# Constant products in TensorE's early gaps, a third head pair turned in float32, and a new order

## The chip, the cores and the metric

One core of one Trainium2 chip. The metric is the device time of one execution in microseconds (us). A kernel's runs are compared by their median. PE stands for TensorE's matmuls, PEld for its weight loads, DVE for VectorE, ACT for ScalarE, POOL for GpSimd, SP for the queue that issues the DMAs.

## The reference, cut to what matters

```python
# q, k, v: (4, 8, 768, 64) float32; proj: (64, 6); w_in: (512, 2048); w_out: (2048, 512)
q_bucket = sum((q @ proj > 0) * 2**arange(6)); k_bucket = the same of k
scores = where(q_bucket == k_bucket, q @ k.T / 8, -1e9)
attn = softmax(scores)              # per batch and head, 768 x 768
x = (attn @ v) as (3072, 512)       # heads side by side
h = x @ w_in
out = (0.5 * h * (1 + erf(h / sqrt(2)))) @ w_out
```

## The kernel before, in words

The work is a list of steps, each with an engine (or several that it may run on), a cost, a sort key out of the table `PAR`, and the steps that it needs. `Plan.order()` walks through them event by event and fixes the order in which every engine's instructions are written; the loop at the end of `tile_bucket_attention_moe` then emits them. On the chip each engine works through its own list in that order and waits on semaphores. So numbers in `PAR` and `HOPX` alone can move any step to another place or engine.

Attention is done in 192 **units**: one head, 128 rows of queries. A unit is: scores on TensorE (`scores`, L764, four matmuls, written to one of two PSUM buffers, s_62 or s_63, of two banks each); the row maximum on VectorE (L767); a guard (L771); the exponential with its row sum on ScalarE (L777); a reciprocal (L786). The weights must then be transposed for the product with the values, in one of two ways:

- *In halves:* VectorE or another engine writes a float16 high part (L396 or L399), VectorE the low part (L792), and the DMA queue transposes both (`turn`). The product with the values (L889) then has three float16 terms: 36 matmuls for two heads and 256 rows. The values too are split into halves (L631 is their low part).
- *Whole* (`whole_turn`): TensorE multiplies the float32 weights by a diagonal matrix of the reciprocals (L832, six matmuls for each unit), and ScalarE or VectorE copies the two halves of the result out of PSUM (`pt<-hp`, L396 or L399). The product with the values (L880) is in float32, 12 matmuls for two heads and 256 rows; the trace shows each float32 matmul as two records.

There are five passes over the units: pass one (rows 0 to 255 of batch 0, units 1 to 16), pass two (the other 512 rows of batch 0, units 17 to 48, the heads in reverse order), and one pass for each of the batches 1 to 3 (units 49 to 192). `WHOLE` says how many of the four head pairs of each pass go the whole way: four in pass one, two in pass two.

Before scores can be made, each head is hashed (`head`: copies, low parts, L719 to L724 on TensorE, signs on ScalarE). Beside the attention of batch 0 the two weight matrices are decoded out of float64 bits on VectorE (L488, L493, L498), their column sums come from TensorE (L510), and they are scaled and split (L558). The feed-forward part is written in groups: L1091 (into the hidden layer), GELU and split, L1158 (out of it). Its matmuls are the only large work that has no successor waiting; TensorE takes them wherever the plan puts them, and about a quarter of the span is left for them at the end, when no attention is left.

The planner keeps a model of TensorE's clock: time is counted in windows, and a step costs double while the window before was not busy enough (`warm`, `window`, `busy`).

Of the kernel before, what the change touches and what calls it, by code (L numbers as in the profile page):

```python
# [24 lines left out]
NEARLY = 2  # L25
RAWE = 1
KEEP = 3
WHOLE = (4, 2, 0, 0, 0)
TABLE = 1.3
WORDER = (("in", 0), ("in", 1), ("out", 0), ("out", 1), ("in", 2), ("in", 3), ("out", 2), ("out", 3))  # L30
GROW = ("p", "hl", "hl", "hl")

PAR = dict(DR_ACT=-376.07, DR_DVE=289.34, SI0=-278.25, SI1=416.6, SI2=306.7, SI_ACT=509.76, SI_DVE=47.66, SI_Pool=-124.88, Z=203.87, VS0=-105.38, H0=492.56, HL=-258.56, VS=-598.47, G2=553.48, HQ=415.51, VQ=-319.5, in0=576.69, out0=43.64, in1=45.59, out1=-9.06, in2=355.85, out2=56.84, in3=-68.45, out3=9.31, H1=322.83, H2=284.27, H3=-599.77, H4=-314.36, H5=134.87, H6=-600, H7=-32.98, MEV=599.38, MGE=18.26, MSP=118.02, V0=600, QK0=-74.85, QK1=593.04, QK2=76.57, MX0=-331.22, MX1=-185.25, MX2=-453.28, EX0=-301.14, EX1=-117.73, EX2=94.64, NR0=-107.13, NR1=-107.34, NR2=-398.77, HI0=584.08, HI1=-88.77, HI2=215.64, LO0=-593.61, LO1=-36.26, LO2=394.43, PV0=336.47, PV1=233.76, PV2=-154.35, TR0=-587.53, TR1=-414.23, TR2=158.02, V1=-484.38, V2=-573.42, Sin0=304.53, Sin1=397.8, Sin2=24.49, Sin3=-283.57, Sout0=471.96, Sout1=295.43, Sout2=26.22, Sout3=336.14, Lin=-221.37, Pin=-423.65, Qin=587.63, Cin=107.98, Min=438.2, Lout=-519.34, Pout=-600, Qout=-600, Cout=-600, Mout=578.13, G0=109.59, G1=-596.66, G3=-600, G4=-600, G5=-286.31, G6=-363.67, G7=-231.43, DUP0=-165.96, DUP1=326.7, DUP2=-339.67, LOW0=420.82, LOW1=-261.59, LOW2=-577.83, PRJ0=282.56, PRJ1=-69.75, PRJ2=-89.26, MSK0=456.41, MSK1=238.81, MSK2=501.82, DI_ACT=-410.83, DI_DVE=252.78, DI_Pool=-258.86, WS_ACT=-29.21, WS_DVE=-440.66, WS_Pool=490.46, WH_ACT=181.51, WH_DVE=-447.36, WH_Pool=-599.06, WL_ACT=70.41, WL_DVE=214, WL_Pool=283.28, VH_ACT=203.1, VH_DVE=477.67, VH_Pool=-442.09, MV_SP=97.35, MV_ACT=338.88, MV_DVE=-2.69, MV_Pool=-599.57, LO_ACT=301.58, LO_DVE=265.1, LO_Pool=-475.84, RND_ACT=-398.89, RND_DVE=200.27, RND_Pool=-52.67, MSK_ACT=48.02, MSK_DVE=-6.3, MSK_Pool=587.68, HI_ACT=-301.94, HI_DVE=128.62, HI_Pool=-390.82, DG_ACT=-447.94, DG_DVE=-318.17, DG_Pool=490.83, EV_ACT=140.3, EV_DVE=-346.2, EV_Pool=-344.6, GH_ACT=361.7, GH_DVE=587.31, GH_Pool=-257.89)
HOPX = {"PE": 0.0, "DVE": -0.1, "ACT": 0.14, "Pool": 0.1, "SP": 0.93}
BIG = 2.0**34
TINY = 2.0**-120

# [16 lines left out]
class Plan:  # L54
# [39 lines left out]
    def order(self):  # L94
# [26 lines left out]
        free_at.update(self.START)  # L121
        dma_at, table = 0.0, "exp"
        port_at, port_of = 0.0, None
        warm, window, busy = False, 0, {}
        mode = 0
        for t in set(free_at.values()):
            heapq.heappush(events, (t, -1, None))
# [1 line left out]
        while events:  # L129
            now, _, ended = heapq.heappop(events)  # L130
            batch = [ended]
            while events and events[0][0] <= now:
                batch.append(heapq.heappop(events)[2])
            for e in batch:
                if e is None:
                    continue
                for hold in e.frees:
                    hold["left"] -= 1
                    if not hold["left"]:
                        at_ = now + self.HOP[e.engine]  # L140
                        self.rings[hold["holder"].takes].append((hold["holder"].slot, at_))
                        heapq.heappush(events, (at_, -1, None))
                for u in users.get(e, ()):
                    left[u] -= 1
                    for w in u.ways:
                        hop = self.SAME.get(w, 0.05) if w == e.engine else self.HOP[e.engine] + HOPX.get(e.engine, 0.0) + 0.12 * (w == "Pool")
                        at[u, w] = max(at.get((u, w), 0.0), now + hop)
                        heapq.heappush(events, (at[u, w], -1, None))
                    if not left[u]:
                        enlist(u)  # L150
            for engine, pool in ready.items():
                if free_at[engine] > now or not pool:
                    continue
                best = None
                for s in pool:
                    if at.get((s, engine), 0.0) > now:
                        continue
                    if s.takes and not (self.rings[s.takes] and self.rings[s.takes][0][1] <= now):
                        continue
                    if engine == "SP" and len(s.ways) > 1 and dma_at > now + self.QUEUE:  # L160
                        continue
                    held = engine == "Pool" or (engine == "DVE" and s.port)
                    if held and port_of != engine and port_at > now:
                        continue
                    rank = (s.key + s.ways[engine][1], s.seq)
                    if best is None or rank < best_rank:
                        best, best_rank = s, rank
                if best is None:
                    continue
                s = best  # L170
                for e in s.ways:
                    ready[e].remove(s)
                s.engine, s.cost = engine, s.ways[engine][0]
                if s.takes:
                    s.slot = self.rings[s.takes].pop(0)[0]
                    head[s.takes] += 1
                    if head[s.takes] < len(queues[s.takes]):
                        after = queues[s.takes][head[s.takes]]
                        if after in waiting:
                            waiting.remove(after)  # L180
                            enlist(after)
                s.start = now
                cost = s.cost
                if s.table and s.table != table:
                    cost += TABLE
                    table = s.table
                if engine == "PE":
                    cost += self.SWITCH[mode][s.mode]
                    mode = s.mode
                    while window < int(now / self.WINDOW):  # L190
                        share = busy.get(window, 0.0) / self.WINDOW
                        warm = share > (0.35 if warm else 0.8)
                        window += 1
                    cost *= 1 if warm else 2
                    a, z = now, now + cost
                    while a < z:
                        w = int(a / self.WINDOW + 1e-9)
                        b = min(z, (w + 1) * self.WINDOW)
                        busy[w] = busy.get(w, 0.0) + b - a
                        a = b  # L200
                if engine == "SP":
                    free_at[engine] = now + s.issue
                    dma_at = max(dma_at, now + 1.0) + cost
                    if dma_at > now + self.QUEUE:
                        heapq.heappush(events, (dma_at - self.QUEUE, -1, None))
                    s.end = dma_at + 0.75
                else:
                    free_at[engine] = s.end = now + cost
                    if engine == "Pool" or (engine == "DVE" and s.port):
                        port_at, port_of = s.end - self.PORT, engine  # L210
                        heapq.heappush(events, (port_at, -1, None))
                count += 1
                heapq.heappush(events, (free_at[engine], -1, None))
                heapq.heappush(events, (s.end, s.seq, s))
# [8 lines left out]
def tile_bucket_attention_moe(  # L223
# [10 lines left out]
    nc = tc.nc  # L234
# [102 lines left out]
    ident = const.tile([P, P], BF16, tag="ident", name="ident")  # L337
    make_identity(nc, ident)
    ones = const.tile([P, P], BF16, tag="ones", name="ones")
    nc.gpsimd.memset(ones, 1.0)  # L340
    warm = const.tile([P, 1], F32, tag="warm", name="warm")
    nc.scalar.activation(out=warm, in_=ones[:, :1], func=AF.Exp)
    limit = const.tile([P, 2], F32, tag="limit", name="limit")
    nc.gpsimd.memset(limit, BIG / 2)
    SPARE = 1000
    for t in bufs["s"]:
        nc.vector.memset(t[:, SPARE : SPARE + 1], 1.0)

# [13 lines left out]
    for n, rr in enumerate((slice(0, D), slice(D, P))):  # L362
        nc.vector.tensor_tensor(
            out=hash_lo[rr, n * KR : n * KR + 2 * NBIT], in0=praw[rr],
            in1=hash_hi[rr, KR : KR + 2 * NBIT].bitcast(F32), op=ALU.subtract,
        )

    plan = Plan(rings)
# [594 lines left out]
    for n_pass, (b, chunks) in enumerate(passes):  # L963
# [9 lines left out]
        for pos, h in enumerate(heads):  # L973
# [14 lines left out]
            _, _, base, made = owner[i]  # L988
# [255 lines left out]
```

## Time and profile before

| | |
|---|---|
| median of 3 runs | 907.84 us (907.3 to 909.52) |
| the profiled execution | 907.79 us, of which 906.0 us are the span from the first instruction to the last |
| PE busy | 865.1 us, 95% |
| DVE busy | 693.8 us, 77% |
| ACT busy | 618.9 us, 68% |
| POOL busy | 275.4 us, 30% |
| mean granted TensorE clock | 0.987 |

The busy shares are means over two very different stretches: up to about 680 us attention runs, with the feed-forward part between its steps; after it only the feed-forward part is left, and the page's row of tenths shows VectorE at one or two tenths there.

### The profile page before, as it was taken

What the parts mean: (1) busy time and instruction counts of PE and PEld (TensorE: products, weight loads), DVE (VectorE), ACT (ScalarE), POOL (GpSimd) and SP (SyncE); (2) the same over time, 40 slices, a digit from 0 to 9 for tenths busy, and PEclk for the clock granted to TensorE, in tenths of its full rate; (3) what the DMA queues carried; (4) which work ended last, traced back from release to release, by engine and by line L of the source; (5) the groups of instructions that cost most, each with busy time, mean ns of one, the idle gap of its engine ahead of it and who ended that gap; (6) DMA issues with size and microseconds to landing.
All of it is one profiled execution on the core that took longest, in us unless ns stands there. A gap on an engine that the chain in (4) does not pass through costs nothing. (4 is left out here: it accounts for less than half of the span.)

```text
span 906.0 us, 17437 instructions
## 1 busy us (share of the span) xinstructions
PE 865.1 (95%) x6592; PEld 630.8 (70%) x6592; DVE 693.8 (77%) x1334; ACT 618.9 (68%) x1028; POOL 275.4 (30%) x282
## 2 busy tenths in 40 slices
PE   4779999799999999999999999999999999999997
PEld 3557878565776867678776766777776757676663
DVE  7899999999999999998999998899994121212112
ACT  5777879878798888887888779878875323232231
POOL 6441134535455333333543324443510000000000
PEclk9969999899999999999999999999999999999999
DMA  8754563769989889997998988999796000000000
GB/s 255 229 161 153 182 219 90 141 140 185 193 197 205 160 204 204 178 184 156 209 182 198 203 158 181 174 194 162 159 162 100 25 11 14 24 1 25 1 24 24
DMA packets 299973, 128.30 MB, mean 142 GB/s; under 512 B 254064, under 2 KB 281840, under 8 KB 299888
## 3 DMA queue, kind: packets, MB, share of 16 engines
q1 hardware_dynamic: 299712, 127.17, 64.7%
q8 instruction: 52, 0.85, 0.4%
q14 instruction: 33, 0.27, 0.1%
q10 hardware_dynamic: 176, 0.00, 0.0%
HBM read 45.49 MB, written 6.29 MB: 57 GB/s over the span
## 5 line engine op out<-in xcount | busy, mean ns | idle before, releaser
L1091 PE MATMUL hp<-x,Win 128*128 128x256 f16 x2304 | 269.4, 274 | 0.0
L1158 PE MATMUL hp<-Wout,g 128*128 128x512 f16 x1152 | 265.6, 380 | 0.0
L1091 PEld LDWEIGHTS <-Win 128*128 128x128 f16 x2304 | 220.8, 98 | 43.3 <-issue 12.8
L1158 PEld LDWEIGHTS <-g 128*128 128x128 f16 x1152 | 107.5, 98 | 125.0 <-issue 10.4
L767 DVE TENSOR_REDUCE s<-s 128x1 f32<-128x768 f32 x192 | 180.8, 955 | 6.9 <-PE s L764 6.1
L777 ACT ACTIVATE p<-s,rows 128x768 f32<-128x768 f32 x141 | 139.2, 987 | 31.9 <-DVE rows L771 17.2
L764 PE MATMUL s<-Ak,Aq 128*128 128x384 f32 x352 | 139.4, 396 | 14.0 <-ACT p L777 8.5
L1101 ACT ACTIVATE h<-hp,ffs 128x512 f32<-128x512 f32 x96 | 65.6, 684 | 120.7 <-PE hp L1091 120.5
L1139 DVE SCALAR_TENSOR_TENSOR g<-h,ffs,g 128x512 f16<-128x512 f32 x96 | 71.4, 760 | 71.6 <-ACT g L396 68.1
L764 PE MATMUL s<-Bk,Bq 128*128 128x384 f32 x352 | 121.6, 345 | 0.0
L764 PEld LDWEIGHTS s<-Ak,Aq 128*128 128x128 f32 x352 | 68.5, 195 | 38.9 <-ACT p L777 14.1
L889 PE MATMUL hp<-pt,vhl 128*64 128x256 f16 x1440 | 85.5, 274 | 1.0 <-DVE x L916 1.0
L399 DVE TENSOR_SCALAR g<-h,ffs 128x512 f16<-128x512 f32 x36 | 19.5, 541 | 86.6 <-PE hp L1158 80.8
L889 PEld LDWEIGHTS <-vhl 128*64 128x64 f16 x1440 | 76.1, 110 | 11.8 <-issue 10.8
L764 PEld LDWEIGHTS s<-Bk,Bq 128*128 128x128 f32 x352 | 69.0, 196 | 1.0
L792 DVE SCALAR_TENSOR_TENSOR wbits<-p,rows,wbits 128x768 f16<-128x768 f32 x63 | 65.8, 1052 | 1.5 <-ACT wbits L396 0.7
L419 POOL TENSOR_TENSOR Bk<-raw,Aq 64x768 fp32r<-64x768 f32 x30 | 58.6, 1953 | 26.0 <-ACT Aq L396 20.8
L399 POOL TENSOR_SCALAR rows<-rows 128x1 f32<-128x1 f32 x57 | 23.3, 408 | 114.5 <-ACT p L777 72.3
L777 ACT ACTIVATE wbits<-s,rows 128x768 f32<-128x768 f32 x51 | 50.4, 988 | 10.2 <-DVE rows L771 6.8
L832 PE MATMUL hp<-dr,p 128*128 128x128 f32 x384 | 51.7, 288 | 3.1 <-ACT dr L396 2.3
L832 PEld LDWEIGHTS hp<-dr,p 128*128 128x128 f32 x384 | 48.1, 200 | 8.4 <-ACT dr L396 4.4
L727 ACT ACTIVATE sign<-hp,off 44x256 f32<-44x256 f32 (+1 forms) x74 | 41.6, 571 | 16.7 <-PE hp L724 16.3
(161 smaller groups left out, 1198.2 us busy)
## 6 DMA issues: line engine op xcount, KB each, us to landing
raw<-qk SPq DMA_DIRECT2D x33, 384.0 KB, 4.0
vraw<-v SPq DMA_DIRECT2D x30, 384.0 KB, 4.1
wbits<-w_in SPq DMA_DIRECT2D x16, 512.0 KB, 4.4
wbits<-w_out SPq DMA_DIRECT2D x16, 512.0 KB, 4.2
out<-o SPq DMA_DIRECT2D x12, 512.0 KB, 3.5
Ak<-Aq SPq DMA_DIRECT2D x24, 192.0 KB, 3.4
Bk<-Aq SPq DMA_DIRECT2D x19, 192.0 KB, 3.2
vhl<-v SPq DMA_DIRECT2D x6, 384.0 KB, 5.1
```

The costliest lines, as they stand in the source:

```text
L399: on.tensor_scalar(out=out, in0=in_, scalar1=scale, scalar2=bias, op0=ALU.mult, op1=ALU.add)
L419: on.tensor_tensor(out=out, in0=in0, in1=in1, op=ALU.subtract)
L764: nc.tensor.matmul(to, x, y, start=k == 0, stop=k == 1)
L767: nc.vector.tensor_reduce(out=buf(sp)[:, SPARE + 1 : SPARE + 2], in_=both(sp), axis=AX.XY, op=ALU.max, negate=True)
L777: nc.scalar.activation(out=buf(ex).rearrange("p (b k) -> p b k", b=2), in_=both(sp), func=AF.Exp, scale=sc, bias=nb, accum_out=ssum,)
L792: nc.vector.scalar_tensor_tensor(out=buf(hi)[:, 1], in0=buf(ex), scalar=r, in1=buf(hi)[:, 0], op0=ALU.mult, op1=ALU.subtract,)
L832: nc.tensor.matmul(buf(step[0])[:, (k - k0) * P : (k - k0 + 1) * P], buf(ex)[:, words(k)], buf(dg), start=True, stop=True,)
L889: nc.tensor.matmul(pv[j * D : (j + 1) * D], buf(vh)[:, tv, kt, j * D : (j + 1) * D], buf(holds[j][0])[:, tp * KT + kt, :nt], start=kt == 0 ...
L1091: nc.tensor.matmul(buf(pair[0])[:, j * ch[1] : (j + 1) * ch[1]], win_hl[:, f0 // WB1, tw, pr, f0 % WB1 : f0 % WB1 + P], x[:, tx, pr, : ch[1]],
L1101: nc.scalar.activation(out=bufs["h"][0][:, 2 * fp : 2 * fp + 2, :nt], in_=buf(pair[0])[:, : 2 * nt].rearrange("p (j k) -> p j k", j=2), fu ...
L1139: nc.vector.scalar_tensor_tensor(out=gt[:, 1, s2, :nt], in0=h[:, s2, :nt], scalar=sg, in1=gt[:, 0, s2, :nt], op0=ALU.mult, op1=ALU.subtract,)
L1158: nc.tensor.matmul(buf(banks[u]), gt[:, tg, f, u * P : (u + 1) * P], wout_hl[:, ft // UT, tw, ft % UT], start=fresh and f == ti == 0, stop ...
```

## The change: what it does

1. `WHOLE` becomes (4, 3, 0, 0, 0). The third head pair of pass two (heads 3 and 2, units 33 to 40) goes the whole way.
2. The emitting loop writes products of two constants (`ones` and `ident`, 128 x 124, bfloat16) ahead of a TensorE step wherever the plan has a gap there before its time 100: 0.6 of the gap's length is filled, counted at 0.058 us for a product, in the first gap at twice that. They go to columns 896 to 1019 of the first score buffer (s_62), which nothing reads; `SPARE` moves from 1000 to 1020 to make room.
3. The planner's model of the clock is gone: every step costs the same at any time.
4. `PAR` has new numbers throughout, and two of `HOPX` change, so the whole order is another.

```diff
-WHOLE = (4, 2, 0, 0, 0)
+WHOLE = (4, 3, 0, 0, 0)
-PAR = dict(DR_ACT=-376.07, DR_DVE=289.34, SI0=-278.25, ...
-HOPX = {"PE": 0.0, "DVE": -0.1, "ACT": 0.14, "Pool": 0.1, "SP": 0.93}
+PAR = dict(DR_ACT=424.31, DR_DVE=-91.59, SI0=26.89, ...
+HOPX = {"PE": 0.0, "DVE": -0.1, "ACT": 0.14, "Pool": 0.06, "SP": 1.04}
...
+    FILL = (2.3, 100.0, 0.058, 0.6)
...
-                    while window < int(now / self.WINDOW):
-                        share = busy.get(window, 0.0) / self.WINDOW
-                        warm = share > (0.35 if warm else 0.8)
-                        window += 1
-                    cost *= 1 if warm else 2
...
-    SPARE = 1000
+    SPARE = 1020
...
     steps = plan.order()
+    idle, until, one, share = plan.FILL
     with tc.manual_schedule():
         for s in steps:
+            if s.engine == "PE":
+                if s.start < until:
+                    cold = 2 if idle == plan.FILL[0] else 1
+                    for _ in range(int((s.start - idle) * share / (one * cold))):
+                        nc.tensor.matmul(
+                            bufs["s"][0][:, 896:SPARE], ones, ident[:, : SPARE - 896], start=True, stop=True,
+                            skip_group_check=True,
+                        )
+                idle = s.end
             s.emit()
```

What the built programs hold, counted: 198 constant products in 16 bursts; float32 turning products (L832) 192 before and 240 now; float32 value products 96 and 120; float16 value products 1440 and 1368; DMA transposes 160 and 152; instructions on POOL 287 and 248, on ACT 841 and 877, on DVE 1336 and 1347. Lines after the planner are 11 lower in the changed kernel (L764 becomes L753, L832 L821, L767 L756, L880 L869).

**Two places in the order.** The first is TensorE between the turning of units 3 and 4 and the hash of the third head (its operands are x_103 and rest), early in pass one; hp is PSUM, dr the diagonal, p the exponentials. Before:

```order
L832 MATMUL hp_67<-dr_118,p_69 128x128 [waits Activation_49]
L832 MATMUL hp_67<-dr_118,p_69 128x128 x2
L832 MATMUL hp_65<-dr_118,p_69 128x128 [waits DVE_49]
L832 MATMUL hp_65<-dr_118,p_69 128x128 x2
L719 MATMUL hp_66<-x_103,hash_lo 44x256
```

Now, at the same place, the first of 23 constant products, and after the last of them the hash:

```order
L821 MATMUL hp_66<-dr_118,p_69 128x128 [waits Activation_49]
L821 MATMUL hp_66<-dr_118,p_69 128x128 x2
L821 MATMUL hp_67<-dr_118,p_69 128x128 x3
L1202 LDWEIGHTS ones
L1202 MATMUL s_62<-ident,ones 128x124 [waits Activation_49]
...
L708 MATMUL hp_64<-x_103,hash_lo 44x256 [waits Pool_49]
```

The burst's first product waits for ScalarE: followed back, for the exponential that reads s_62, the last user of the buffer that the products write to. So the burst, and the hash behind it, start after that exponential.

The second place is VectorE around the row maxima (TENSOR_REDUCE) of units 37 and 38 in pass two, where the third pair stands. Before:

```order
L792 SCALAR_TENSOR_TENSOR hl_70<-p_68,rows,hl_70 128x768
L488 TENSOR_SCALAR Wout<-wbits 128x512 x2
L493 SCALAR_TENSOR_TENSOR Wout<-wbits,Wout 128x512 x2
L498 SCALAR_TENSOR_TENSOR Wout<-wbits,Wout 128x512 x2
L786 RECIPROCAL rows<-rows 128x1
L771 SCALAR_TENSOR_TENSOR rows<-limit,s_62 128x2
L399 TENSOR_SCALAR hl_71<-p_69,rows 128x768
L767 TENSOR_REDUCE s_63<-s_63 128x1
L792 SCALAR_TENSOR_TENSOR hl_71<-p_69,rows,hl_71 128x768
```

Now:

```order
L756 TENSOR_REDUCE s_62<-s_62 128x1
L388 TENSOR_SCALAR pt_75<-hp_66 128x3x128
L760 SCALAR_TENSOR_TENSOR rows<-limit,s_62 128x2
L388 TENSOR_SCALAR pt_75<-hp_67 128x3x128
L669 SCALAR_TENSOR_TENSOR Bq_90<-raw_78,Aq_88 64x512
L775 RECIPROCAL rows<-rows 128x1
L547 SCALAR_TENSOR_TENSOR Win<-Wout,tiny,Win 128x1024
```

The low parts (L792) and the high part (L399 into hl) of the pair's units are gone from VectorE, and copies of turned weights (pt) stand there; parts of the weights' scaling have moved behind them.

More of the change, by code (lines that the diff above doesn't have):

```diff
@@ L31 @@
 GROW = ("p", "hl", "hl", "hl")
-PAR = dict(DR_ACT=-376.07, DR_DVE=289.34, SI0=-278.25, SI1=416.6, SI2=306.7, SI_ACT=509.76, SI_DVE=47.66, SI_Pool=-124.88, Z=203.87, VS0=-105.38, H0=492.56, HL=-258.56, VS=-598.47, G2=553.48, HQ=415.51, VQ=-319.5, in0=576.69, out0=43.64, in1=45.59, out1=-9.06, in2=355.85, out2=56.84, in3=-68.45, out3=9.31, H1=322.83, H2=284.27, H3=-599.77, H4=-314.36, H5=134.87, H6=-600, H7=-32.98, MEV=599.38, MGE=18.26, MSP=118.02, V0=600, QK0=-74.85, QK1=593.04, QK2=76.57, MX0=-331.22, MX1=-185.25, MX2=-453.28, EX0=-301.14, EX1=-117.73, EX2=94.64, NR0=-107.13, NR1=-107.34, NR2=-398.77, HI0=584.08, HI1=-88.77, HI2=215.64, LO0=-593.61, LO1=-36.26, LO2=394.43, PV0=336.47, PV1=233.76, PV2=-154.35, TR0=-587.53, TR1=-414.23, TR2=158.02, V1=-484.38, V2=-573.42, Sin0=304.53, Sin1=397.8, Sin2=24.49, Sin3=-283.57, Sout0=471.96, Sout1=295.43, Sout2=26.22, Sout3=336.14, Lin=-221.37, Pin=-423.65, Qin=587.63, Cin=107.98, Min=438.2, Lout=-519.34, Pout=-600, Qout=-600, Cout=-600, Mout=578.13, G0=109.59, G1=-596.66, G3=-600, G4=-600, G5=-286.31, G6=-363.67, G7=-231.43, DUP0=-165.96, DUP1=326.7, DUP2=-339.67, LOW0=420.82, LOW1=-261.59, LOW2=-577.83, PRJ0=282.56, PRJ1=-69.75, PRJ2=-89.26, MSK0=456.41, MSK1=238.81, MSK2=501.82, DI_ACT=-410.83, DI_DVE=252.78, DI_Pool=-258.86, WS_ACT=-29.21, WS_DVE=-440.66, WS_Pool=490.46, WH_ACT=181.51, WH_DVE=-447.36, WH_Pool=-599.06, WL_ACT=70.41, WL_DVE=214, WL_Pool=283.28, VH_ACT=203.1, VH_DVE=477.67, VH_Pool=-442.09, MV_SP=97.35, MV_ACT=338.88, MV_DVE=-2.69, MV_Pool=-599.57, LO_ACT=301.58, LO_DVE=265.1, LO_Pool=-475.84, RND_ACT=-398.89, RND_DVE=200.27, RND_Pool=-52.67, MSK_ACT=48.02, MSK_DVE=-6.3, MSK_Pool=587.68, HI_ACT=-301.94, HI_DVE=128.62, HI_Pool=-390.82, DG_ACT=-447.94, DG_DVE=-318.17, DG_Pool=490.83, EV_ACT=140.3, EV_DVE=-346.2, EV_Pool=-344.6, GH_ACT=361.7, GH_DVE=587.31, GH_Pool=-257.89)
@@ L34 @@
-HOPX = {"PE": 0.0, "DVE": -0.1, "ACT": 0.14, "Pool": 0.1, "SP": 0.93}
+PAR = dict(DR_ACT=424.31, DR_DVE=-91.59, SI0=26.89, SI1=289.76, SI2=-328.27, SI_ACT=335.37, SI_DVE=-535.28, SI_Pool=502.17, Z=21.77, VS0=-400.31, H0=596.97, HL=-600, VS=306.25, G2=148.65, HQ=593.83, VQ=408.04, in0=564.34, out0=246.97, in1=128.09, out1=-230.97, in2=-38.81, out2=40.55, in3=120.35, out3=140.08, H1=582.74, H2=238.66, H3=-543.26, H4=-473.58, H5=-388.5, H6=-594.88, H7=239.72, MEV=-538.16, MGE=600, MSP=-272.87, V0=199.33, QK0=-96.48, QK1=-68.18, QK2=-190.2, MX0=-346.49, MX1=-514.56, MX2=-348.69, EX0=-293.88, EX1=-165.44, EX2=149.78, NR0=-174.26, NR1=-409.56, NR2=250.52, HI0=600, HI1=-337.54, HI2=585.12, LO0=-471.86, LO1=205.82, LO2=364.71, PV0=448.31, PV1=482.37, PV2=-314.77, TR0=-588.47, TR1=-346.7, TR2=-31.15, V1=-50.2, V2=-585.86, Sin0=600, Sin1=416.59, Sin2=470.62, Sin3=-358.29, Sout0=499.9, Sout1=562.92, Sout2=56.57, Sout3=583.63, Lin=511.46, Pin=502.88, Qin=421.66, Cin=519.51, Min=579.03, Lout=541.2, Pout=-319.56, Qout=-14.32, Cout=-167.85, Mout=-96.1, G0=87.94, G1=-131.68, G3=-553.2, G4=-600, G5=58.72, G6=-600, G7=-558.83, DUP0=-105.72, DUP1=-192.91, DUP2=-441.6, LOW0=429.02, LOW1=-109.17, LOW2=-506.91, PRJ0=349.57, PRJ1=-182.31, PRJ2=287.51, MSK0=225.06, MSK1=-589.95, MSK2=596.41, DI_ACT=-597.38, DI_DVE=-190.79, DI_Pool=-23.37, WS_ACT=-367.67, WS_DVE=533.76, WS_Pool=-212.64, WH_ACT=6.84, WH_DVE=600, WH_Pool=-238.36, WL_ACT=-91.81, WL_DVE=-204.9, WL_Pool=-479.88, VH_ACT=-186.43, VH_DVE=334.32, VH_Pool=468.01, MV_SP=600, MV_ACT=165.52, MV_DVE=241.86, MV_Pool=-461.71, LO_ACT=-558.03, LO_DVE=-218.86, LO_Pool=-557.28, RND_ACT=387.83, RND_DVE=-4.59, RND_Pool=-25.32, MSK_ACT=115.47, MSK_DVE=39.09, MSK_Pool=-142.03, HI_ACT=-522.3, HI_DVE=-243.04, HI_Pool=-293.04, DG_ACT=-212.43, DG_DVE=36.12, DG_Pool=-502.03, EV_ACT=-362.4, EV_DVE=-292.37, EV_Pool=-374.68, GH_ACT=276.5, GH_DVE=-545.1, GH_Pool=309.84)
@@ L123, in order @@
         port_at, port_of = 0.0, None
-        warm, window, busy = False, 0, {}
         mode = 0
@@ L189, in order @@
                     mode = s.mode
-                    while window < int(now / self.WINDOW):
-                        share = busy.get(window, 0.0) / self.WINDOW
-                        warm = share > (0.35 if warm else 0.8)
-                        window += 1
-                    cost *= 1 if warm else 2
[L195 to L200, printed above, removed]
                 if engine == "SP":
```

## The prediction

> **What bounds the kernel now.** I read the page first: span, busy engines, and the tenths of PE, DVE and the granted clock.
>
> ```profile
> span 906.0 us, 17437 instructions
> PE 865.1 (95%) x6592; PEld 630.8 (70%) x6592; DVE 693.8 (77%) x1334; ACT 618.9 (68%) x1028; POOL 275.4 (30%) x282
> PE   4779999799999999999999999999999999999997
> DVE  7899999999999999998999998899994121212112
> PEclk9969999899999999999999999999999999999999
> ```
>
> TensorE looks like the bound (95%), but its row has holes in the first eight slices, and there VectorE is full. So I asked for the busy time by stretches (columns: length, busy PE, PEld, DVE, ACT, POOL, clock, DMA share, GB/s).
>
> ```profile
> 0.00:22.00 22.00, 10.41 (x38) 7.95 (x39) 16.00 (x31) 12.62 (x20) 13.44 (x23) 1.00 0.83 262
> 22.00:46.00 24.00, 17.98 (x137) 13.87 (x135) 21.64 (x51) 17.86 (x37) 10.58 (x9) 1.00 0.75 227
> 46.00:64.00 18.00, 12.83 (x53) 10.19 (x54) 16.35 (x30) 12.86 (x22) 7.46 (x7) 0.53 0.48 140
> 64.00:158.00 94.00, 91.69 (x722) 74.00 (x720) 92.78 (x210) 76.11 (x160) 27.96 (x29) 1.00 0.54 163
> 158.00:172.00 14.00, 10.06 (x78) 7.35 (x74) 13.90 (x24) 13.28 (x19) 6.79 (x4) 1.00 0.93 179
> 172.00:180.00 8.00, 6.77 (x30) 5.45 (x31) 7.84 (x13) 5.94 (x10) 6.40 (x7) 0.57 0.46 96
> 180.00:264.00 84.00, 79.29 (x613) 56.02 (x612) 82.08 (x162) 67.58 (x114) 38.99 (x36) 1.00 0.87 178
> 264.00:371.00 107.00, 106.90 (x855) 78.14 (x854) 101.73 (x195) 91.09 (x150) 42.71 (x47) 1.00 0.93 190
> 371.00:681.00 310.00, 308.76 (x2535) 231.70 (x2534) 292.28 (x548) 251.98 (x420) 120.62 (x123) 1.00 0.91 178
> 681.00:906.00 225.00, 220.39 (x1547) 146.14 (x1545) 49.19 (x79) 69.59 (x85) 0.44 (x1) 1.00 0.10 24
> ```
>
> From 64 to 264 us VectorE is busy 196.6 of 200 us and TensorE 187.8: VectorE sets the pace of the units. From 264 us on TensorE is busy 636.0 of 642 us: whatever feed-forward work is not done by then costs its full time at the end. The seam is unit 64, whose row maximum is the second of this pair:
>
> ```profile
> 262.60 1.80 DVE L767 TENSOR_REDUCE s<-s 128x1 f32<-128x768 f32 x2
> ```
>
> So the change is worth two things: when unit 64 comes, which VectorE sets, and how much feed-forward work TensorE has done by then. Extra TensorE work in the early part is free only where TensorE was idle.
>
> **The change part by part.** *TensorE, the third pair.* The prices are distances from one row's start to the next one's:
>
> ```profile
> 72.06 1.50 PE L832 MATMUL hp<-dr,p 128*128 128x128 f32 x12
> 73.49 1.08 PE L880 MATMUL hp<-pt,vhl 128*64 128x256 f32 x8
> ...
> 120.66 2.81 PE L880 MATMUL hp<-pt,vhl 128*64 128x256 f32 x24
> 123.40 1.60 PE L832 MATMUL hp<-dr,p 128*128 128x128 f32 x12
> ...
> 611.03 2.08 PE hp L889 x36
> 613.11 0.91 PE s L764 x4
> ...
> 736.73 9.71 PE hp L1158 x45
> 746.45 10.48 PE hp L1091 x96
> ```
>
> A unit's turning takes 1.43 us, eight units 11.4. Value products: two blocks of 2.74 in place of two of 2.08, +1.3. Together **+12.7 us** of TensorE work between units 33 and 48, which is 158 to 209 us in the old trace. The idle time of TensorE from 158 to 264 us is 3.94 + 1.23 + 4.71 = 9.9 us, and of the 6.77 busy us at clock 0.57 about 2.9 are the slow clock's, so most of it, not all, can go into holes there; the rest pushes feed-forward matmuls back unless VectorE's pace leaves room earlier.
>
> *Feed-forward work done by unit 64.* Counted in the order ahead of unit 64's scores: 300 matmuls of the first layer (L1091) before, 336 now; 96 of the second (L1158) before, 102 now; hash, weight sums and scores alike. At 10.48/96 = 0.109 us and 9.71/45 = 0.216 us that is 3.9 + 1.3 = **5.2 us** of work done earlier, which the stretch after no longer has to do.
>
> *VectorE up to unit 64.* Means of the groups (busy, mean ns):
>
> ```profile
> L792 DVE SCALAR_TENSOR_TENSOR hl<-p,rows,hl 128x768 f16<-128x768 f32 x46 | 48.0, 1045 | 0.4 <-issue 0.2
> L399 DVE TENSOR_SCALAR pt<-hp 128x384 f32<-128x384 f32 x19 | 10.4, 551 | 3.4 <-PE hp L832 3.2
> L399 DVE TENSOR_SCALAR g<-h,ffs 128x512 f16<-128x512 f32 x36 | 19.5, 541 | 86.6 <-PE hp L1158 80.8
> L680 DVE SCALAR_TENSOR_TENSOR Bq<-raw,Aq 64x768 fp32r<-64x768 f32 (+2 forms) x30 | 37.0, 1234 | 0.9
> ```
>
> Nine low parts fewer (-9.4), nine copies of turned weights more (+5.0), five high parts of the hidden layer more (+2.7), three subtractions that stood on POOL (no such row on DVE; between the 0.55 of a copy and the 1.23 of the low part of a head, I take the nearest in kind, 1.23: +3.7), and small ones that cancel to +0.4. Sum +2.4 us. The same sum of means over all of VectorE's work to unit 64 gives 283.7 us before, where the stretches show 250.6 busy: rows overlap. So +2.4 becomes **+2.1 us**. The relief of VectorE that the third pair could bring is spent on work that the new order takes from POOL; with the three subtractions at 0.55 it would be +0.3, and if all three lay off VectorE's way -1.1.
>
> *The constant products.* Cost of one, from eight products of the same size in bfloat16 with their weight loads, at the full clock and at half of it:
>
> ```profile
> 107.50 0.62 PE L510 MATMUL hp<-Wout 128*128 128x128 bf16 x8
> 107.95 0.62 PE L510 MATMUL hp<-Win 128*128 128x128 bf16 x8
> 108.41 1.55 PE L832 MATMUL hp<-dr,p 128*128 128x128 f32 x12
> ...
> 19.33 1.08 PE L510 MATMUL hp<-Win 128*128 128x128 bf16 x8
> 20.20 2.57 PE L832 MATMUL hp<-dr,p 128*128 128x128 f32 x12
> ```
>
> 0.45/8 = 57 ns, and 0.87/8 = 109 ns. Of the 198, 76 wait for nothing late (32 of them ahead of the first hash, 24 behind it) and run while TensorE was idle anyway. The other 122 stand behind a wait: seven bursts (108 products) for an exponential of s_62, three (14) for VectorE's reading of s_62. They start when that has ended, and the step behind them is next in TensorE's queue. Bounds: nothing, where that step waits longer still; 122 x 0.057 = 7.0 us, where each was ready. The Trainium skill (TensorE: Matmul & The Clock Gate, Back-to-back issue gap) has 81 ns for a matmul of 128 columns with its weight load in a stream; the trace has 57. By the page's figure the upper bound would be 9.9 us.
>
> What they can buy: the clock. The stretch from 46 to 64 us ran at 0.53, and before 22 us the same scores took 0.52 us that take 0.34 later; but VectorE sets the pace, so only its own waits for TensorE count:
>
> ```profile
> DVE s L767 <- PE s L764: 6.1, 13, 1.0
> DVE pt L399 <- PE hp L832: 3.2, 4, 1.6
> ```
>
> 9.3 us in the whole span, of which I put half before 70 us, where TensorE has its holes; at the double clock half of that goes: a gain of 2.3 us, between 0 and 4.6. For the delay I take a third of 7.0 us, 2.3, since VectorE has decoding to do meanwhile (DVE idle to 64 us is 10.0, 6.0 of it before 22). **The two cancel: 0.**
>
> *Nothing on the path:* eight DMA transposes fewer (no wait of TensorE in the list ends in a DMA), the 36 instructions more on ACT (busy 206.3 us of the first 264; its cover is VectorE, and gone if ACT's share passes VectorE's), the end of the program, which has the same 90 matmuls last.
>
> **Sum:** +2.1 - 5.2 + 0 = -3.1 us, against the profiled 907.79 (span 906.0 and 1.8 around it; the median is 907.84, the same): **904.7 us**. About 0.3%, 2.7 us, is what a measurement of this kernel tells from no change.
>
> **The rivals.**
>
> *The bursts cost more than they buy (slower).* Place: TensorE's queue up to unit 25, ten bursts behind waits. If all of 7.0 us lands ahead of unit 64 and the clock buys nothing, the time is 904.7 + 7.0 = 911.7; at the half clock (109 ns, if the products don't hold it up: the change not doing what it says) up to 13.3, 918. It decides from 5.8 us of delay on. For it: the next scores into s_62 need the same exponential, so the burst of 27 ahead of unit 3 begins just when they could. Against it: VectorE's decoding fills such time.
>
> *The lead is lost again (no change).* Ahead of unit 96's scores the order has 576 and 576 matmuls of the first layer, 243 and 240 of the second. If VectorE, with 5 us to spare of 107 before, sets the pace there too, the lead of 5.2 us is not kept, and what counts is its sum to unit 96, 399.0 before and 397.3 now, -1.7 x 0.88 = -1.5: 906.3.
>
> *The wait at 170 us goes too (faster).* TensorE's longest stall after the start is here:
>
> ```profile
> 173.23 0.69 PE L764 MATMUL s<-Ak,Aq 128*128 128x384 f32 x1 [3.45 <-ACT p L777]
> ```
>
> It also lets the clock fall to 0.57 for 8 us, worth 3.4. In the new order turning products stand at this place. With that stretch at full clock and the early gain of 2.3 not paid back: 904.7 - 3.4 - 2.3 = 899.0. A rule of the Trainium skill speaks for the early gain (TensorE: Matmul & The Clock Gate, What's actually happening: a window of about 3.4 us of work lifts the clock). The first 32 products, 3.5 us at 109 ns, would reach it before the first hash; no run here shows it.
>
> **How the numbers follow.** My forecast 0.40, within 901 to 906.5 (a tenth of the whole, 0.04, is above 905.1 and so within 0.3%); the lead lost 0.25; the wait gone too 0.15; the bursts dear 0.20, of which a tenth stays within 0.3%. Faster: 0.36 + 0.15 = 0.51; same: 0.25 + 0.04 + 0.02 = 0.31; slower: 0.18. The range from 898 to 912 takes in all but the dearest bursts and a gain beyond the third rival.
>
> **What would show each step.** Right: the row maximum of unit 64 at about 265 us, TensorE above 99% after it; 480 turning records (384 before) at 1.43 us a unit; constant products in 16 bursts at 57 ns, clock 1.00 from about 15 us to 264. Wrong: if unit 64 comes before 262 us (VectorE's sum mis-sized or its idle time shrunk) or after 268 (bursts, ACT); if TensorE has idle time of more than 4 us between 264 and 371 (the lead lost); if a stretch at half clock remains between 25 and 100 us (the products don't hold it). What would make the whole wrong is a new wait in the second half, where the order is new too and VectorE has only 18 us to spare of 310.

## The result and the profile after

The changed kernel is slower: 916.36 us median (915.94 to 918.41) against 908.68 us for the kernel before on the same chip, a ratio of 1.0089 (95% interval 1.0065 to 1.0113). The prediction was 904.7 us. The page of the profiled execution (916.37 us) begins so: span, busy time of the engines, then busy tenths of TensorE and VectorE and the granted clock in 40 slices.

```profile
span 914.6 us, 17949 instructions
PE 881.8 (96%) x6862; PEld 646.1 (71%) x6862; DVE 704.3 (77%) x1345; ACT 632.5 (69%) x1064; POOL 243.6 (27%) x243
PE   6989999899999999999999999999999999999997
DVE  6979999999999999998999899799698551212112
PEclk9999999999999999999999999999999999999999
```

The holes in TensorE's row are nearly filled and its clock is full almost throughout; the time is longer all the same. Busy time by the same stretches as before (length, PE, PEld, DVE, ACT, POOL, clock, DMA share, GB/s):

```profile
0.00:22.00 22.00, 13.07 (x112) 11.48 (x113) 15.18 (x29) 11.60 (x21) 12.29 (x21) 0.92 0.79 248
22.00:46.00 24.00, 21.76 (x202) 18.22 (x200) 22.11 (x49) 18.30 (x37) 9.58 (x10) 1.00 0.70 204
46.00:64.00 18.00, 14.18 (x107) 11.03 (x108) 13.56 (x23) 11.31 (x20) 7.51 (x8) 0.91 0.59 176
64.00:158.00 94.00, 90.71 (x740) 74.55 (x738) 92.00 (x216) 75.22 (x160) 22.78 (x22) 1.00 0.55 168
158.00:172.00 14.00, 12.82 (x95) 10.24 (x93) 13.94 (x22) 11.48 (x24) 7.38 (x7) 1.00 0.24 57
172.00:180.00 8.00, 6.42 (x50) 5.21 (x47) 8.00 (x16) 6.08 (x13) 3.08 (x2) 1.00 0.36 116
180.00:264.00 84.00, 81.75 (x618) 57.84 (x618) 82.55 (x161) 67.83 (x109) 26.28 (x27) 1.00 0.69 150
264.00:371.00 107.00, 106.40 (x858) 78.62 (x855) 102.59 (x195) 90.86 (x151) 50.25 (x50) 1.00 0.92 190
371.00:681.00 310.00, 306.06 (x2448) 225.02 (x2447) 276.32 (x505) 247.33 (x406) 92.42 (x87) 1.00 0.83 164
681.00:914.60 233.60, 228.58 (x1651) 153.88 (x1648) 78.00 (x136) 92.48 (x132) 11.98 (x12) 1.00 0.21 47
```

The clock column counts all time ahead of the first rise of the clock as full: before, that rise came at 22.3 us (eight products at 19.3 us took 0.87 us, half speed), now it comes at 5.5 us. From 46 to 64 us the clock is 0.91 where it was 0.53, yet VectorE has done less: 13.6 us of work against 16.4. From 158 to 264 us TensorE idles 5.0 us instead of 9.9. The row maxima of units 64 and 96 on VectorE:

```profile
270.01 0.96 DVE L756 TENSOR_REDUCE s<-s 128x1 f32<-128x768 f32 x1
...
373.40 0.94 DVE L756 TENSOR_REDUCE s<-s 128x1 f32<-128x768 f32 x1
```

Unit 64 comes 6.5 us later than before (263.5), where 265 was forecast, and unit 96 2.6 us later (370.8 before). The first loss lies where the products stand. TensorE between 57 and 62 us (start, length, the idle time ahead and its releaser in brackets):

```profile
57.06 0.63 PE L499 MATMUL hp<-Wout 128*128 128x128 bf16 x8
...
60.02 2.13 PE L1202 MATMUL s<-ident,ones 128*128 128x124 bf16 x20 [2.33 <-ACT p L766]
61.91 0.45 PE L708 MATMUL hp<-Aq,hash_lo 128*44 128x256 f32 x1
```

The hash of L708 would have been next in the queue. The products ahead of it write unread columns of the score buffer s_62 and wait for the exponential that reads the same buffer. The Trainium skill (PSUM — Partial Sum Buffer, PSUM bank collisions raise a hardware error) says to guard that memory with semaphores by bank and group of 32 partitions, and not by address; columns that nobody reads, in a bank that is being read, then wait like any others. The 2.33 us here agree with that; whether the guard stands on the bank or on the whole buffer can't be told from them.

### The profile page after: what moved, and what is told of

It reads as the page before. It is cut to its first block, busy times and chain, and to the rows that moved or that the text cites. A ratio compares the mean times of both kernels' runs of the same rounds, so it can differ in the third digit from the quotient of the medians.

```text
span 914.6 us, 17949 instructions
## 1 busy us (share of the span) xinstructions
PE 881.8 (96%) x6862; PEld 646.1 (71%) x6862; DVE 704.3 (77%) x1345; ACT 632.5 (69%) x1064; POOL 243.6 (27%) x243
## 5 line engine op out<-in xcount | busy, mean ns | idle before, releaser
L1147 PE MATMUL hp<-Wout,g 128*128 128x512 f16 x1152 | 265.1, 380 | 0.0
L756 DVE TENSOR_REDUCE s<-s 128x1 f32<-128x768 f32 x192 | 180.5, 955 | 13.6 <-PE s L753 9.6
L753 PE MATMUL s<-Ak,Aq 128*128 128x384 f32 x352 | 135.8, 386 | 4.4 <-ACT p L766 2.5
L1128 DVE SCALAR_TENSOR_TENSOR g<-h,ffs,g 128x512 f16<-128x512 f32 x96 | 77.6, 824 | 64.5 <-ACT g L385 58.4
L753 PE MATMUL s<-Bk,Bq 128*128 128x384 f32 x352 | 118.5, 337 | 0.0
L753 PEld LDWEIGHTS s<-Ak,Aq 128*128 128x128 f32 x352 | 66.2, 188 | 25.4 <-ACT p L766 8.1
L878 PE MATMUL hp<-pt,vhl 128*64 128x256 f16 x1368 | 80.3, 274 | 0.9 <-DMA pt<-wbits 0.6
L878 PEld LDWEIGHTS <-vhl 128*64 128x64 f16 x1368 | 72.7, 110 | 9.8 <-issue 9.8
L753 PEld LDWEIGHTS s<-Bk,Bq 128*128 128x128 f32 x352 | 66.5, 189 | 1.0
L821 PE MATMUL hp<-dr,p 128*128 128x128 f32 x480 | 63.0, 279 | 3.6 <-ACT dr L385 1.9
L821 PEld LDWEIGHTS hp<-dr,p 128*128 128x128 f32 x480 | 58.1, 191 | 9.3 <-ACT dr L385 3.1
L408 POOL TENSOR_TENSOR Bk<-raw,Aq 64x768 fp32r<-64x768 f32 x28 | 53.6, 1913 | 33.0 <-ACT Aq L385 17.9
L766 ACT ACTIVATE wbits<-s,rows 128x768 f32<-128x768 f32 x50 | 49.3, 987 | 12.7 <-DVE rows L760 7.0
L716 ACT ACTIVATE sign<-hp,off 44x256 f32<-44x256 f32 (+1 forms) x74 | 41.6, 570 | 13.6 <-PE hp L713 11.5
```

The lines of the kernel that those rows point to most:

```text
L408: on.tensor_tensor(out=out, in0=in0, in1=in1, op=ALU.subtract)
L753: nc.tensor.matmul(to, x, y, start=k == 0, stop=k == 1)
L756: nc.vector.tensor_reduce(out=buf(sp)[:, SPARE + 1 : SPARE + 2], in_=both(sp), axis=AX.XY, op=ALU.max, negate=True)
L766: nc.scalar.activation(out=buf(ex).rearrange("p (b k) -> p b k", b=2), in_=both(sp), func=AF.Exp, scale=sc, bias=nb, accum_out=ssum,)
L821: nc.tensor.matmul(buf(step[0])[:, (k - k0) * P : (k - k0 + 1) * P], buf(ex)[:, words(k)], buf(dg), start=True, stop=True,)
L878: nc.tensor.matmul(pv[j * D : (j + 1) * D], buf(vh)[:, tv, kt, j * D : (j + 1) * D], buf(holds[j][0])[:, tp * KT + kt, :nt], start=kt == 0 ...
```

## Experiments

Three theories stood against each other: the bursts of constant products are dear (B), the third pair's work finds no room on TensorE (P), or the new order is itself slower (O). Ratios are to the kernel before on the same chip, with 95% intervals.

**The changed kernel without products.**

```diff
-    FILL = (2.3, 100.0, 0.058, 0.6)
+    FILL = (2.3, 0.0, 0.058, 0.6)
```

> The changed kernel with the constant products left out, nothing else moved (they are no part of the result). Theory B, the bursts are dear: they take 15.1 us of TensorE's time and replace 8.1 us of its idle time, so without them about 7 us come back, 909 to 911, although the clock falls to half somewhere before 64 us. Theory P, the third pair's 12.7 us of TensorE work find no room: the products only keep the clock up, and without them the half clock returns (11 us of slower records in the kernel before), 917 to 925. Theory O, the new order is worse in itself: 914 to 918, since early idle time is then traded for late.

Measured: 909.39 us, 1.0028 (1.0011 to 1.0045). Its row maxima of units 64 and 96:

```profile
265.14 0.96 DVE L756 TENSOR_REDUCE s<-s 128x1 f32<-128x768 f32 x1
...
368.89 0.94 DVE L756 TENSOR_REDUCE s<-s 128x1 f32<-128x768 f32 x1
```

Theory B's range was met and theory P's was not, and something of theory O holds too: the products cost 0.6% (5.5 us), and the order with its third pair alone is 0.28% (2.5 us) slower instead of 0.3% faster. Unit 64 is at 265.1, as forecast for the whole change; unit 96 is 1.9 us ahead of before. TensorE around the hash:

```profile
56.67 0.63 PE L499 MATMUL hp<-Wout 128*128 128x128 bf16 x8
57.11 0.31 PE L708 MATMUL hp<-Aq,hash_lo 128*44 128x256 f32 x1
```

The hash starts at 57.1 us instead of 61.9.

**The products alone, in the order of before** (197 of them by its own plan).

```diff
+    FILL = (2.3, 100.0, 0.058, 0.6)
...
-    SPARE = 1000
+    SPARE = 1020
...
+                    for _ in range(int((s.start - idle) * share / (one * cold))):
+                        nc.tensor.matmul(bufs["s"][0][:, 896:SPARE], ones, ident[:, : SPARE - 896], ...
```

> The kernel before with the constant products alone, placed in the gaps of its own plan: 197 of them, of which 51 stand behind a wait. Theory B: what waits costs at most 51 x 0.057 = 2.9 us, and the clock that the rest holds up gives back some, 904 to 911. Theory P and theory O: the products do no harm and the clock's 11 us of slower records partly go, 902 to 907. A stretch at half clock that remains between 25 and 100 us speaks against the products altogether.

Measured: 909.06 us, 1.0004 (0.9979 to 1.0030): nothing gained. Busy time from 46 to 64 us there:

```profile
46.00:64.00 18.00, 11.76 (x90) 10.03 (x91) 16.98 (x29) 12.86 (x22) 7.90 (x8) 0.81 0.55 161
```

The clock rose from 0.53 to 0.81 and VectorE did 17.0 us of work instead of 16.4; by unit 96 nothing is left of it (371.0 us). The median hides a spread that goes with the clock: the three executions with a mean granted clock of 0.986 or 0.987 took 909.7 to 911.1 us, the three with 0.993 to 0.996 took 904.8 to 906.0. The kernel before does the same: of 31 executions on one chip the eight at 0.985 or less took 907.8 to 911.6 us, the ten at 0.989 or more 903.1 to 907.7. Which of the two, time or clock, brings the other is not shown.

**Two pairs again, with and without products; three pairs in the old order.**

```diff
-WHOLE = (4, 3, 0, 0, 0)
+WHOLE = (4, 2, 0, 0, 0)
```

With the products:

> The changed kernel with two head pairs of pass two turned in float32, as before; products and new numbers stay. Theory P: 12.7 us of work less on TensorE, 903 to 907. Theory B: the bursts stay as they are, and units 33 to 40 cost VectorE 9 low parts again: 912 to 917. Theory O: 914 to 918.

Without them:

> The new numbers and the planner without its clock, with two pairs and without the constant products: the order alone. Theory O: 912 to 917, with TensorE idle for 8 us or more from 264 us on. Theory P: 903 to 907. Theory B: 905 to 909.

The kernel before with (4, 3):

> The kernel before with three head pairs of pass two turned in float32 and nothing else; the old numbers, the plan drawn anew with them. The pair adds 12.7 us of work to TensorE. With two and three pairs the new numbers gave 915.6 and 909.4 without products, the pair there a gain of 6, since TensorE waited 19 us from 158 to 264 with two. The old numbers leave 9.9 us of waits there: if the pair fills waits only, the rest shows, 908 to 912; if it is a loss as in my sum's first term, 915 to 921; if it is a gain by itself, 901 to 905.

Measured: 927.40 us, 1.0208 (1.0154 to 1.0262); 915.63 us, 1.0088 (1.0053 to 1.0122); 929.82 us, 1.0247 (1.0216 to 1.0278). The first and the third lie outside all that was expected; the second met theory O's time, with 6.8 us of idle TensorE from 264 us on where 8 or more were expected. With the new numbers the third pair is worth 6 us without products and 11 us with them, and with the old ones it costs 23 us. So it is not the extra work alone that decides. From 158 to 264 us, first the version with three pairs and no products, then that with two pairs and none:

```profile
158.00:264.00 106.00, 101.09 (x760) 73.51 (x759) 104.34 (x197) 85.28 (x143) 35.58 (x38) 1.00 0.65 141
```

```profile
158.00:264.00 106.00, 86.71 (x623) 59.43 (x621) 100.72 (x192) 82.05 (x132) 41.31 (x34) 0.94 0.77 159
```

With two pairs TensorE idles 19.3 us there and its clock drops; with the third pair it idles 4.9 us and is busy 14.4 us more, near the 12.7 us of the pair's work. With the old numbers the pair does not cost its 23 us where it stands. Unit 64 comes at 260.5 us there, 2.9 earlier than before, and unit 96 at 372.5, 1.7 later; 22.0 us are lost from there to the end (the kernel before takes 535.18 us with 4081 records there, shown further down):

```profile
372.52:929.70 557.18, 547.78 (x4190) 388.10 (x4188) 353.56 (x634) 333.81 (x522) 114.78 (x117) 1.00 0.55 109
```

Of the 109 TensorE records more, 69 are of the first layer and 40 of the second, 16 us by the prediction's prices, and TensorE idles 3.6 us longer. The plan drawn anew had put feed-forward work off to the end; why it did is open. With these two sets of numbers, the third pair pays only with the new ones.

**Which bursts.** In the order of the queue there are 17, not 16 as counted ahead of the prediction: of 32, 24, 27, 2, 23, 7, 8, 1, 1, 24, 4, 20, 6, 6, 6, 6 and 1 products. The first two alone, and all but these:

```diff
+                    count = int((s.start - idle) * share / (one * cold))
+                    bursts += count > 0
-                    for _ in range(int((s.start - idle) * share / (one * cold))):
+                    for _ in range(count if bursts <= 2 else 0):
```

> The changed kernel with its first two bursts alone (56 products, all ahead of the first scores, behind no late wait). Theory B (what stands behind a wait or ahead of a ready step is paid in full): they are free and lift the clock some microseconds earlier, so the time is that of the kernel without products or up to 2 us less, ratio to before 1.001 to 1.003. The other reading, that any product costs its 57 to 109 ns somewhere: 56 of 198 of the cost, ratio 1.004 to 1.006.

> The changed kernel without its first two bursts (the other 142 products stay). Theory B: nearly the whole cost stays, ratio 1.007 to 1.010. The other reading: 142 of 198 of the cost and a later clock, ratio 1.005 to 1.007.

Measured: 910.63 us, 1.0041 (1.0020 to 1.0061) with 56 products; 915.30 us, 1.0092 (1.0075 to 1.0109) with 142. The first lies in the range of the other reading, though its interval reaches into theory B's; the second is theory B's. Most of the cost is behind the second burst. Then without the bursts of 27, 2 and 20 (the third, fourth and twelfth), where the trace shows TensorE held up, and with these alone (the same edit, with `bursts not in (3, 4, 12)` and `bursts in (3, 4, 12)`):

> The changed kernel without three of its bursts (27 ahead of unit 3, 2 ahead of unit 4, 20 ahead of a hash after unit 12: 49 of 198 products). In the trace these hold up a step that was ready: the 2 stand behind unit 3's row maximum while unit 4's scores need only an older exponential, the 20 behind an exponential that the hash doesn't need. If the cost lies there: row maximum of unit 96 at 369 to 371 us (373.4 with all, 368.9 with none) and ratio to before 1.002 to 1.005. If the cost is spread with the number of products: 372.3 us, ratio 1.007 to 1.008.

> The reverse: those three bursts alone, 49 products. If the cost lies there: unit 96 at 372 to 374 us, ratio 1.006 to 1.009. If it is spread: 370 us, ratio 1.003 to 1.005.

Measured: 910.13 us, 1.0030 (1.0015 to 1.0045) with 149 products, as good as none; 914.53 us, 1.0079 (1.0063 to 1.0096) with 49, its unit 96 at 372.2 us. The first one's unit 96, at 371.6 us in its profiled execution, lies outside what was expected, but that execution (912.43 us) was one of the longest of its ten. Three bursts carry nearly all.

**Wait or length.** One product for each burst keeps every wait and drops the length:

```diff
-                    for _ in range(int((s.start - idle) * share / (one * cold))):
+                    for _ in range(min(1, int((s.start - idle) * share / (one * cold)))):
```

> The changed kernel with one product in each burst (17 of them, since one gap that held none to speak of counts too): the waits stay, the length goes. If the cost of a burst is its length behind the wait: as without products, ratio 1.002 to 1.004. If it is the wait itself, which holds up a step that could have run: ratio 1.006 to 1.009.

Measured: 913.83 us, 1.0076 (1.0059 to 1.0094): 17 products of some 54 ns, 1 us in all, cost 0.48%. But its first 22 us ran at a clock of 0.86, so the slow clock could have been the reason. The next four put each product into the buffer that the step behind it takes, so that it waits for nothing that this step would not wait for:

```diff
+                        into = bufs["hp"][s.slot][:, : SPARE - 896] if s.takes == "hp" else (
+                            bufs["s"][s.slot if s.takes == "s" else 0][:, 896:SPARE]
+                        )
-                            bufs["s"][0][:, 896:SPARE], ones, ...
+                            into, ones, ...
```

One for each burst:

> The version with one product for each burst (17 in all), each written into the buffer that the step behind it takes next. Against the 17 with their waits on s_62 (ratio 1.0076): if the wait is the cost, ratio 1.001 to 1.004, as without products; if that version lost its time by the slow clock of its first 26 us, or by the order's changed beginning, ratio 1.006 to 1.009 again.

Measured: 909.56 us, 1.0027 (1.0009 to 1.0045), as without products, at a clock of 0.87 in the first 22 us. TensorE at the hash, first with the waits on s_62, then without them:

```profile
58.52 0.63 PE L499 MATMUL hp<-Wout 128*128 128x128 bf16 x8
61.48 0.21 PE L1202 MATMUL s<-ident,ones 128*128 128x124 bf16 x1 [2.33 <-ACT p L766]
61.51 0.31 PE L708 MATMUL hp<-Aq,hash_lo 128*44 128x256 f32 x1
```

```profile
56.85 0.63 PE L499 MATMUL hp<-Wout 128*128 128x128 bf16 x8
57.32 0.21 PE L1205 MATMUL hp<-ident,ones 128*128 128x124 bf16 x1
57.34 0.31 PE L708 MATMUL hp<-Aq,hash_lo 128*44 128x256 f32 x1
```

And unit 96, in the same sequence:

```profile
372.49 0.94 DVE L756 TENSOR_REDUCE s<-s 128x1 f32<-128x768 f32 x1
```

```profile
368.15 0.94 DVE L756 TENSOR_REDUCE s<-s 128x1 f32<-128x768 f32 x1
```

The same 17 products are 4.3 us apart at unit 96, and only the buffer they write differs: the wait alone is enough for most of the loss. The three dear bursts, and all 198, in the same manner:

> The bursts of 27, 2 and 20 alone (49 products), each in the buffer of the step behind it. Against the same bursts with their waits on s_62 (ratio 1.0079): if the wait is the cost, ratio 1.002 to 1.005, unit 96 at 369 to 371 us; if the length, 1.006 to 1.009, unit 96 at 372 or later.

> The changed kernel, with all 198 constant products, but each written into the buffer that the step behind it takes next, so that a product waits for nothing that this step would not wait for. If the added wait is what the products cost: within 0.2% of the version without products, ratio 1.002 to 1.005, unit 96 at 369 to 371 us, and the hash step at 62 us begins at 59 to 60. If their length is the cost: ratio 1.007 to 1.010, unit 96 at 372 to 374.

Measured: 911.23 us, 1.0051 (1.0031 to 1.0071), against 1.0079 with the waits; 912.13 us, 1.0062 (1.0041 to 1.0082), against 1.0089 (an interval that it overlaps). Both lie between the theories: taking the waits away gives back 0.27 to 0.28%, and the length of the bursts keeps 0.23 to 0.34% (each of these differences is known to some 0.25 to 0.3%). With the 17, the wait alone had cost 0.48%: so the two parts do not simply add up to the whole. The three alone, behind no first two bursts, ran at half speed at their first place:

```profile
16.69 2.81 PE L1208 MATMUL s<-ident,ones 128*128 128x124 bf16 x27 [2.46 <-ACT p L766]
19.27 0.67 PE L753 MATMUL s<-Ak,Aq 128*128 128x384 f32 x1
```

Their unit 96, at 372.1 us in the profiled execution, lies in the range of the length and is no earlier than with the waits; that execution (913.87 us) was the second longest of its twelve. For all 198 the length's share can't be placed: the profiled execution (span 907.8 us, unit 96 at 368.8, the hash at 58.5) was the shortest of nine. In the order of before:

> The kernel before, with the 197 products of its own plan, each in the buffer of the step behind it. With the waits on s_62 they made no difference (1.0004). If the waits took what the clock gave: ratio 0.995 to 0.998, no half clock from 46 to 64 us. If VectorE's pace hides both: 0.999 to 1.002.

Measured: 907.28 us, 0.9993 (0.9973 to 1.0013), in the last of these ranges. The clock was full from 14.8 to 168.4 us. Unit 64 came at 260.8 us in the profiled execution, 2.7 earlier than before, unit 96 at 369.7, 1.1 earlier, and of that 0.2 us was left at the end (span 905.8). So without added waits the products do help there, but no gain is left that the medians show. The clock is no guide to the time here: of the twelve executions those of 902.8 and of 909.7 us both had 0.991.

**Why the order is slower behind unit 96.** Without products, the old numbers for the keys of the batches behind the first, and the old numbers that choose engines, were put back:

```diff
-SI2=-328.27, ... QK2=-190.2, MX2=-348.69, EX2=149.78, ...
+SI2=306.7, ... QK2=76.57, MX2=-453.28, EX2=94.64, ...
```

> No products, three pairs, the new numbers, but with the old ones for the steps of batches 1 to 3 (all keys that end in 2 for scores, maxima, exponentials, weights and values, and the lead of their heads). Without products the new order has unit 96 at 368.9 us, 1.9 before the old one, and still ends 1.3 us after it, so it loses 3 us behind unit 96. If the numbers of batches 1 to 3 lose them: ratio 0.995 to 0.999. If the split of work between engines does, or the plan as a whole: 1.003 or more.

```diff
-... EV_ACT=-362.4, EV_DVE=-292.37, EV_Pool=-374.68, ...
+... EV_ACT=140.3, EV_DVE=-346.2, EV_Pool=-344.6, ...
```

> No products, three pairs, the new numbers, but the old biases for which engine takes a step that may run on several (all keys that end in ACT, DVE, Pool or SP). If the new split, 39 instructions off POOL, is what costs: ratio 0.994 to 1.000. If order and split were drawn together and one without the other fits nothing: 1.005 to 1.03, as the third pair alone did.

Measured: 916.16 us, 1.0096 (1.0081 to 1.0111), and 937.94 us, 1.0328 (1.0289 to 1.0367). Both worse: the numbers fit only each other, and these runs don't separate the cause.

## Why the prediction was wrong

The forecast was 3.1 us faster, the result 7.7 us slower. About half of the difference are the products, the other half is the order.

**The step that failed first: "The two cancel: 0."** The delay was taken as a third of 7.0 us, the clock's gain as 2.3. Measured, the products cost 5.5 us net by the medians (7.3 by the two profiled spans, 914.6 and 907.3). That is the rival "the bursts cost more than they buy", given 0.20 and 911.7 us; its sign and place were right, but it too was priced by length alone. Of the 7.3 us, 4.5 stand at unit 96. The other 2.8 lie behind it, where no product stands: from unit 96 to the end the ten traces of this order with three pairs, with all, some or no products, take 538.4 to 541.2 us, the version without products least and the changed kernel most. What spreads them is open. One term in the step was missing and one was too large.

The missing term is the wait. The delay was priced by length alone, 57 ns for each of 122 products, and a third of it, 2.3 us, was taken; by the versions with own buffers the length does cost some 2 to 3 us net of what the clock gives back. The waits, 0.27 to 0.28% or some 2.5 us in the same versions, had no price. TensorE's waits for products in the changed kernel (total us, times, longest):

```profile
PE s L1202 <- ACT p L766: 7.0, 5, 2.9
...
PE s L1202 <- DVE rows L775: 1.1, 1, 1.1
...
PE s L1202 <- DVE rows L760: 0.7, 1, 0.7
```

8.8 us of waiting that the step behind the product may not need. The prediction had the rows to see it: it listed which bursts wait for an exponential, but asked only whether the next step waits "longer still", not whether it waits for that buffer at all. The scores of unit 3 take s_62 and wait for the same exponential; there the burst's 1.43 us is the added part. First the changed kernel, then that without products:

```profile
17.64 1.62 PE L1202 MATMUL s<-ident,ones 128*128 128x124 bf16 x27 [2.93 <-ACT p L766]
19.07 0.42 PE L753 MATMUL s<-Ak,Aq 128*128 128x384 f32 x1
...
21.07 0.27 PE L1202 MATMUL s<-ident,ones 128*128 128x124 bf16 x2 [1.06 <-DVE rows L775]
21.14 0.42 PE L753 MATMUL s<-Ak,Aq 128*128 128x384 f32 x1
```

```profile
16.67 0.66 PE L753 MATMUL s<-Ak,Aq 128*128 128x384 f32 x1 [2.61 <-ACT p L766]
...
18.09 0.53 PE L753 MATMUL s<-Ak,Aq 128*128 128x384 f32 x1
```

Unit 4's scores, at 21.14, take s_63 and were held 1.06 us for s_62. The hash at 61.9 us takes no score buffer. VectorE pays for it. In the changed kernel it waits for the signs that the late hash feeds; without products the same row maximum starts without a wait:

```profile
64.71 0.97 DVE L756 TENSOR_REDUCE s<-s 128x1 f32<-128x768 f32 x1 [3.49 <-ACT sign L716]
```

```profile
60.74 0.96 DVE L756 TENSOR_REDUCE s<-s 128x1 f32<-128x768 f32 x1
```

Behind these 3.49 us VectorE is the pace up to 264 us (busy 196.5 of the last 200 us), so nothing is made up: 4.0 us here are 4.9 at unit 64.

The clock's gain of 2.3 us was the term too large, for the new order needs little help: without products it keeps the full clock from 51 us to the end, the stretch at 172 us included, so there was little left to buy, and its executions took hardly less time where their clock was higher (909.6 us at 0.993, 909.0 and 909.3 at 0.998); and with them one stretch at half clock remained, at 60 us, which the text had named as a sign against them. That the "wait at 170 us" went was right, and was the order's doing.

**The lead of 5.2 us.** The counts were right, and so was VectorE's term: unit 64 at 265.1 us without products. But the order alone came out 2.5 us slower instead of 3.1 faster. By unit 96 it is 1.9 us ahead, 3.5 of the 5.2 us having shown between units 64 and 96. Then it loses them. From unit 96 to the end, before, without products, and changed:

```profile
370.82:906.00 535.18, 529.33 (x4081) 377.91 (x4079) 341.66 (x628) 321.67 (x505) 121.23 (x124) 1.00 0.57 113
```

```profile
368.89:907.30 538.41, 531.07 (x4085) 377.48 (x4082) 351.47 (x636) 337.83 (x533) 103.37 (x97) 1.00 0.57 114
```

```profile
373.40:914.60 541.20, 532.24 (x4085) 377.17 (x4082) 351.92 (x636) 337.64 (x533) 102.71 (x97) 1.00 0.56 113
```

Without products TensorE's recorded work, four records more (one unit's scores, under 1 us), takes 3.2 us longer, 1.5 of it idle TensorE: small waits, most of them ahead of scores, none over 0.6 us. The traces of the order of before take 535.2 to 536.1 us there, against 538.4 and more, so the loss is more than the spread. The sum had priced no wait there; the text named "a new wait in the second half" only as what would make it wrong. What of the new order causes them stays open. The rival "the lead is lost again" had the lead go, but by another mechanism, and put the time at 906.3, still ahead of before: between 264 and 371 us TensorE idles 0.6 us, so VectorE did not take the lead over.

**Right:** turning in 480 records at 1.39 us a unit,

```profile
160.90 2.84 PE L821 MATMUL hp<-dr,p 128*128 128x128 f32 x24
163.67 1.08 PE L869 MATMUL hp<-pt,vhl 128*64 128x256 f32 x8
```

(2.77 us for two; forecast 1.43 for one); a product, forecast at 57 ns, at 53 (27 in 1.43 us, at full clock); the early clock, full from 12.4 us, but only to 60.2. The upper end, 912, was 4.4 us short: it set the dear bursts against a lead that came in full.

No version tried beats the kernel before. The nearest in the new order are those without products (1.0028) and with one product each in its own buffer (1.0027).

## What to carry to other kernels

Filler work in an in-order queue is not priced by its length alone but also by what it must wait for: give it a buffer whose readers the step behind it has to wait for anyway, or ask of each place whether that step needs the same release. Ask also who sets the pace there: where another engine does, a faster clock on this one can buy little more than that engine's waits for it. And where an order is fitted to its own costs as a whole, a lead counted at one seam is not yet time at the end; look for what the order does behind it, and leave room for a small wait at every place that it newly makes.

## What the runs showed of the hardware

The stretches at half clock behind the first rise last 3.413 us or a multiple of it (3.4, 6.8, 10.2, 17.1) in every trace here, but for the last of each, which the end cuts off. Idle time alone does not say where the clock falls; how it lies across the steps of 3.413 us does. In the changed kernel the clock was at half from 60.2 to 63.6 us, right behind the 2.33 us for which the burst of 20 had stopped the queue. They lie wholly in one step, in which TensorE was busy for 1.08 us (columns as in the tables above):

```profile
56.75:60.16 3.41, 1.08 (x14) 0.66 (x12) 3.38 (x7) 3.14 (x6) 0.91 (x2) 1.00 0.52 182
```

In the version with one product for each burst the same 2.33 us of idle time, up to 61.5 us, are shared by two steps, and neither brought a fall: its clock was full from 26 to 910 us.

```profile
56.76:60.17 3.41, 2.40 (x20) 1.76 (x19) 3.38 (x7) 1.84 (x3) 0.68 (x1) 1.00 0.70 240
60.17:63.58 3.41, 2.10 (x13) 1.83 (x13) 2.46 (x6) 3.35 (x9) 1.15 (x3) 1.00 0.49 136
```

Counted over the 18 traces in steps of 3.413 us from each change of the clock: every step at full clock with a fall behind it had TensorE busy for 1.64 us or less, every one without a fall for 1.52 or more; every step at half clock with a rise behind it had 2.90 us or more, every one without a rise 2.78 or less. The program does not fix where the steps begin: the nine executions of the version with all 198 products in their own buffers had a mean granted clock of 0.995 to 1.000. So a few filler products can't be relied on to hold it.

With the first two bursts (32 products from 1.5 us, 24 from 9.8) the clock was full from 5.5 to 9.0 and again from 12.4 to 60.2 us. In the same order without products the first rise came at 13.2 us, and in the kernel before at 22.3. The Trainium skill (TensorE: Matmul & The Clock Gate, What's actually happening) says that some 3.4 us of work lift the throttle; the first burst of 3.47 us and the rise at 5.5 agree.
